# One-core attention and MLP kernel: the first head pair loaded by tokens, own buffers for q and k, a new order

## The chip, the cores and the metric

The kernel runs on one core of a Trainium2 chip. The metric is the device time of one execution in microseconds (us), taken on the chip; three executions give a median, 614.7 us before the change.

The engines are called by their profile names: PE multiplies matrices, PEld loads PE's stationary operand, DVE, ACT and POOL work element by element, and SP issues nearly all transfers (DMAs). PE writes to PSUM, a small memory of eight banks, from which only ACT and DVE copy.

## The reference

Causal attention over 4 batches x 12 heads x 448 tokens x 64, then a two-layer MLP on the 1792 tokens:

```
scores = q @ k.T / 8, masked above the diagonal
attn   = exp(scores - rowmax) / (rowsum + 1e-9)
x      = (attn @ v), heads side by side            # 1792 x 768, f32
h      = x @ w_in                                  # 768 x 2048
g      = where(h >= 1, h, where(h <= -1, 0, (h + 1)**2 / 4))
out    = g @ w_out                                 # 2048 x 768
```

q, k and v arrive as f32, w_in and w_out as 64-bit floats. The kernel narrows each weight from its two 32-bit words, splits it into a high and a low part and multiplies in three passes. Likewise it splits x and g.

## The kernel before

**Work.** Heads are taken in pairs, 24 of them (4 batches x 6), numbered 0 to 23. For a pair, *prep_pair* loads q and k and turns them so that the 64 head dimensions lie on partitions; *pair* makes the scores on PE (line L820, "S", 28 records of the profile), masks them and takes the row minimum on DVE (L839), takes exp on ACT (L843), scales by the reciprocal sum on POOL, ACT or DVE (L752, L754, L755), transposes the result on PE (L768, "T", 16 records) into a PSUM tile *t*, copies that to *pt* on ACT or DVE (L791, L796), and multiplies by v (L868, "V", 16 records). The result is split into x on ACT and DVE (L471, L480). The seven row tiles of a pair are called e6 (the widest) to e0.

The first MLP layer (*mlp1*, L617) needs the six x tiles of a batch. It runs in triples (the three passes for one block f of 128 columns and one x tile), 96 per batch and 384 in all, between the attention steps of the following batch. Its results pass through ACT (L627), DVE (L630) and either DVE (L636) or POOL (L633, L634) into *r* and are stored to DRAM. Only two *h* banks hold them. The second layer (L984) comes last, 1176 matmuls.

**Weights.** Each block of w_in comes in two transfers of 384 KB, 32 in all, into four raw buffers that are reused. ACT (L500) and DVE (L503, L505) decode, and a split on ACT, DVE or POOL follows. w_out is decoded during the attention, stored to DRAM and read back.

**The first pair.** PE starts with 18 fill matmuls on zeros (L894) and runs 7 more after the first scores. q and k of a pair are each loaded by four DMAs: 32 partitions, 3456 contiguous bytes each, where two bands of 32 dimensions are read by two overlapping loads, so each byte comes twice. A 32x32 transpose on DVE (L718) then makes the 64-row layout. The buffers for these loads are two *st* tiles, shared with the last w_in blocks. Pair 1 uses two early tiles of its own.

**What sets the order.** Nothing is ordered by hand. A planner (*Plan*) holds a list of tasks with costs, dependences and buffers. It simulates the engines with its own cost figures (*mm*, *act*, *dve*, *dma*), and after a first ranking it replays a list of seeds (STEPS), each of which shakes the priorities, the PE order or the engine chosen for some tasks. What comes out is the fixed order of every engine and of SP's queue. Each engine takes its instructions strictly in that order, so one that waits holds up all behind it. SP's transfers too are issued in order: one that waits for a buffer holds back the later ones.

Of the kernel before, what the change touches and what calls it, by code (L numbers as in the profile page):

```python
# [49 lines left out]
class Plan:  # L50
# [99 lines left out]
    def solve(self):  # L150
# [4 lines left out]
        for ahead in (14.0,):  # L155
            for pen in (0.1,):
# [204 lines left out]
def kernel(  # L361
# [9 lines left out]
    nc = tc.nc  # L371
# [23 lines left out]
    EVEN = 5  # L395
    NSTG = 2
# [8 lines left out]
        "w": 2 * KF, "st": 2, "sr": 2, "wn": 4, "x": 9, "r": 3, "vv": 1, "h": 2,  # L405
        "qs": 4, "vr": 2, "pt": 2,
        **{f"p{i}": 1 for i in range(NI)}, 
        "mn": 4, "su": 4, "s": 4, "t": 2,
        "w2": 8, "z": 2, "hl": 3, "w3": 10, "ot": 2,
# [12 lines left out]
    open_pools(base, "w st sr wn")  # L422
# [4 lines left out]
    open_pools(attn, "qs vr pt mn su")  # L427
# [28 lines left out]
    plan = Plan(slots, {"st", "t"})  # L456
# [52 lines left out]
    def parts(u):  # L509

        if isinstance(u, list):
            return [(x, 0, lambda x=x: x.tile) for x in u]
        if u.tag == "st":
            return [(u, z, lambda z=z: u[:, z * W2:(z + 1) * W2]) for z in range(2)]
        return [(u, z, lambda z=z: u[:, z]) for z in range(2)]
# [20 lines left out]
    def load_w_in(f, behind):  # L536
        w = wi[f] = [buf("w", [P, 2, W2], F32R) for _ in range(2)]
        for c, u in enumerate(w):
            src = w_in[c * K2 * P:(c + 1) * K2 * P, f * 2 * P:(f + 1) * 2 * P]
            if f < KF - NSTG:  # L540
                raw, claim = raw_in(stages[(2 * f + c) % len(stages)]), []
            else:
                raw, claim = raw_in(buf("st", [P, ROW])), [(u, "to")]
# [38 lines left out]
    HOMES = ["w2"] * 8 + ["wn", "wn", "st", "st", "sr", "sr"] + ["w"] * 32 + ["w3"] * 10  # L582

    def unit():
# [3 lines left out]
        if tag == "st":  # L588
            return buf("st", [P, ROW], F32R)
# [20 lines left out]
    def mlp1(b, f, nom):  # L610
        h = buf("s" if b == B - 1 and f >= OPEN else "h", [P, 512])
        for kk in range(KD):
# [9 lines left out]
            task([("PE", mm(S, times=3), go)], 0.0,  # L622
# [76 lines left out]

    def prep_pair(b, p, prio):  # L700
# [3 lines left out]
        for g in range(2):  # L704
            t = head[g] if no == 1 else buf("st", [P, ROW])
            first = None
            for i in range(2):
                row = (q, k)[g][b, 2 * p + i]
                for z in range(2):
# [3 lines left out]
                             dma(32 * 2 * S * 4, 230.0 if no else 185.0), 0.465, lat=1.25 if no else 1.0, early=no == 0, writes=[(t, 2 * i + z)], behind=loads[-1:] if first is None else ())  # L713
# [3 lines left out]
        for g, t in enumerate(nat):  # L717
            task([("DVE", 0.81, lambda g=g, t=t: nc.vector.transpose(  # L718
# [344 lines left out]
```

## Time and profile before

| | us |
|---|---|
| median of 3 runs (lowest, highest) | 614.7 (613.19, 617.15) |
| the profiled execution's own time | 615.45 |
| its span, first to last instruction | 613.6 |
| PE busy | 590.1 |
| DVE busy | 459.7 |
| ACT busy | 311.6 |
| POOL busy | 186.6 |

The span is what the trace covers. The execution's own time is 1.85 us longer, and it lies 0.75 us above the median. A row of a timeline gives start, length, engine, line and operation of a merged group, and in brackets the idle time of the engine before it with what ended it. Matmuls overlap in their pipeline, so the time that PE loses is read from its idle brackets and from the starts of successive groups, and the busy share says little.

### The profile page before, as it was taken

Reading aid. Unit: us, or ns where it says so; the run is one execution under the profiler, and the core shown is the slowest. Engines: PE = TensorE matmul, PEld = TensorE weight load, DVE = VectorE, ACT = ScalarE, POOL = GpSimd, SP = SyncE. Lnnn points to the kernel's source line nnn. Section 1 sums busy time; section 2 is a strip of 40 time slices with the busy share of each in tenths; the row PEclk is TensorE's granted clock in tenths of the full one; section 3 lists DMA queues with packets and bytes.
Section 4 is the critical chain, followed back from the end, with each engine's and each line's share of the span. In section 5 each row is a group of like instructions: output and inputs, shape, how many; then the busy total and the mean of one; then the engine's idle time right before and its main releaser. Section 6 shows DMA issues by size and latency. Waiting matters only on the chain.

```text
span 613.6 us, 11591 instructions
## 1 busy us (share of the span) xinstructions
PE 590.1 (96%) x3793; PEld 512.5 (84%) x3793; DVE 459.7 (75%) x1211; ACT 311.6 (51%) x784; POOL 186.6 (30%) x249
## 2 busy tenths in 40 slices
PE   8887999998999999999999999999999999999997
PEld 5555788776787787687787789999999999999997
DVE  5997999979847876968466779979766676655664
ACT  4997876848525655946356648444212222312221
POOL 2334563464433234120636323451021000032200
PEclk9999999999999999999999999999999999999999
DMA  8767898665887877767776369746323232423331
GB/s 206 220 191 201 249 261 258 179 177 164 209 287 217 277 228 218 193 217 220 206 237 187 99 201 348 241 138 207 107 76 122 75 120 73 135 76 114 91 100 67
DMA packets 96588, 110.33 MB, mean 180 GB/s; under 512 B 33552, under 2 KB 86288, under 8 KB 96528
## 3 DMA queue, kind: packets, MB, share of 16 engines
q1 hardware_dynamic: 96336, 109.15, 59.7%
q8 instruction: 30, 0.49, 0.3%
q10 hardware_dynamic: 192, 0.44, 0.2%
q14 instruction: 30, 0.25, 0.1%
HBM read 78.36 MB, written 31.20 MB: 179 GB/s over the span
## 4 chain that ended last, share of the span: by engine, by line
PE 47%; POOL 2%; DVE 1%; ACT 0%; issue 0%; POOLq 0%; ACTq 0%; DVEq 0%
PE s L984 17%; PE s L617 8%; PE h L984 8%; PE t L984 8%; PE h L617 3%; PE t L768 1%; PE t L868 1%; POOL r L633 1%; POOL r L634 1%; ACT e L843 0%; DVE vv L630 0%; DVE x L480 0%; DVE s L839 0%; PE s L820 0%; POOL su L849 0%
## 5 line engine op out<-in xcount | busy, mean ns | idle before, releaser
L617 PE MATMUL h<-x,w 128*128 128x448 f32 x900 | 204.4, 373 | 3.1 <-DVE vv L630 2.9
L617 PEld LDWEIGHTS h<-x,w 128*128 128x128 f32 x900 | 161.4, 188 | 18.3 <-DVE vv L630 6.1
L471 ACT ACTIVATE hl<-z 128x896 fp32r<-128x896 f32 x49 | 46.7, 952 | 120.7 <-DVE z L480 96.5
L984 PE MATMUL s<-w,hl 128*128 128x384 f32 x534 | 101.3, 335 | 0.0
L984 PEld LDWEIGHTS s<-w,hl 128*128 128x128 f32 x534 | 93.5, 188 | 0.1
L843 ACT ACTIVATE e<-s,mn 128x320 f32<-128x320 f32 (+6 forms) x168 | 78.4, 475 | 29.0 <-DVE mn L839 27.6
L480 DVE TENSOR_TENSOR hl<-z,hl 128x896 fp32r<-128x896 f32 x53 | 58.2, 1099 | 45.3 <-ACT hl L471 40.7
L839 DVE CUSTOM_DVE_ANT_0 s<-s,mask 128x320 f32<-128x320 f32 (+6 forms) x168 | 67.9, 445 | 6.7 <-PE s L820 3.2
L768 PE MATMUL t<-ident,e 128*128 128x128 f32 (+1 forms) x384 | 58.8, 278 | 11.7 <-ACT pt L791 4.7
L768 PEld LDWEIGHTS t<-ident,e 128*128 128x128 f32 (+1 forms) x384 | 43.0, 139 | 26.3 <-POOL e L752 6.3
L480 DVE TENSOR_TENSOR z<-z 128x128 f32<-128x128 f32 x199 | 56.5, 318 | 9.5 <-DMA z<-g_scratch 5.5
L630 DVE TENSOR_TENSOR vv<-h,r 128x448 f32<-128x448 f32 x50 | 31.0, 619 | 40.3 <-ACT r L627 25.2
L627 ACT ACTIVATE r<-h,half 128x448 f32<-128x448 f32 x50 | 31.5, 634 | 51.8 <-PE h L617 45.4
L481 POOL TENSOR_TENSOR z<-z 128x128 f32<-128x128 f32 x25 | 13.1, 524 | 137.2 <-DVE z L480 62.4
L868 PE MATMUL t<-pt,vr 128*64 128x448 f32 (+3 forms) x384 | 50.1, 391 | 3.7 <-ACT e L843 2.1
L984 PE MATMUL h<-w,hl 128*128 128x384 f32 x258 | 52.8, 335 | 0.0
L984 PE MATMUL t<-w,hl 128*128 128x384 f32 x258 | 52.6, 335 | 0.0
L633 POOL TENSOR_SCALAR r<-r 128x448 f32<-128x448 f32 x20 | 36.2, 1808 | 52.7 <-DVE vv L630 51.9
L617 PE MATMUL s<-x,w 128*128 128x448 f32 x252 | 51.8, 363 | 0.0
L868 PEld LDWEIGHTS t<-pt,vr 128*64 128x64 f32 (+1 forms) x384 | 23.9, 135 | 32.8 <-issue 19.9
L617 PEld LDWEIGHTS s<-x,w 128*128 128x128 f32 x252 | 47.0, 188 | 3.0
L984 PEld LDWEIGHTS h<-w,hl 128*128 128x128 f32 x258 | 45.5, 188 | 0.0
(93 smaller groups left out, 840.8 us busy)
## 6 DMA issues: line engine op xcount, KB each, us to landing
g_scratch<-r SPq DMA_DIRECT2D x64, 224.0 KB, 2.9
z<-g_scratch SPq DMA_DIRECT2D x56, 256.0 KB, 2.8
sr<-in_moe_w_out_dram SPq DMA_DIRECT2D x32, 384.0 KB, 4.2
w<-in_moe_w_in_dram SPq DMA_DIRECT2D x28, 384.0 KB, 5.0
w_scratch<-wn SPq DMA_DIRECT2D x56, 192.0 KB, 3.5
st<-in_q_dram SPq DMA_DIRECT2D x90, 108.0 KB, 2.7
st<-in_k_dram SPq DMA_DIRECT2D x90, 108.0 KB, 2.9
w<-w_scratch SPq DMA_DIRECT2D x50, 192.0 KB, 4.1
```

The source lines that it names most:

```text
L471: "ACT": ("ACT", act(n, 0.04), lambda: nc.scalar.activation(out=dst(), in_=src(), func=ACTF.Copy)),
L480: "DVE": ("DVE", dve(n), lambda: nc.vector.tensor_tensor(out=dst(), in0=x(), in1=y(), op=op), port),
L481: "POOL": ("POOL", pool_tt(n), lambda: nc.gpsimd.tensor_tensor(out=dst(), in0=x(), in1=y(), op=op), True),
L617: nc.tensor.matmul(out=h[:, :S], lhsT=wi[f][kk // K2][:, a, kk % K2 * P:(kk % K2 + 1) * P], rhs=x[:, c], start=(kk == 0 and n == 0), stop= ...
L627: task([("ACT", act(S, 0.1), lambda: nc.scalar.activation(out=r.tile, in_=h[:, :S], func=ACTF.Relu, scale=0.5, bias=half[:, 0:1]))], g0, r ...
L630: task([("DVE", dve(S), lambda: nc.vector.tensor_tensor(out=y.tile, in0=h[:, :S], in1=r.tile, op=ALU.max))], g0, reads=[(h, 0), (r, 0)], w ...
L633: nc.gpsimd.tensor_scalar(out=r.tile, in0=r.tile, scalar1=1.0, scalar2=1.0, op0=ALU.min, op1=ALU.mult)
L768: nc.tensor.transpose(t[:k, c:c + P], es[i][:, j * P:j * P + k], turners[i in SWAPPED])
L839: task([("DVE", dve(n) + (0.05 if n < 384 else 0.02), lambda s=s, off=off, n=n, i=i: nc.vector.tensor_tensor_reduce(out=s[:, off:off + n], ...
L843: task([("ACT", act(n, 0.19), lambda s=s, off=off, n=n, i=i: nc.scalar.activation(out=es[i][:, :n], in_=s[:, off:off + n], func=ACTF.Exp, ...
L868: nc.tensor.matmul(out=o[64 * g:64 * g + 64, j * P:S], lhsT=vr[:k, j, g, :], rhs=pt[:k, 7 * j:5 * j + NI, g, :] if j < NJ - 1 else pt[:k, ...
L984: nc.tensor.matmul(out=acc[x][:, :NO], lhsT=hl[:, a, i * P:(i + 1) * P], rhs=(hi, lo)[c](), start=(f == 0 and n == 0), stop=(f == KF - 2 a ...
```

## The change

Pair 0 (LIGHT = 1) now loads q and k by tokens: two DMAs each of 128 partitions x 4 x 64 elements, each run 256 bytes. Four transposes on PE for q and four for k (L729 of the changed kernel) put the layout into PSUM, and a copy on ACT or DVE (L732, L733) brings it to SBUF. q and k have four buffers of their own (*sq*), *vr* has three instead of two, *st* is gone; the last w_in blocks use *sr*, and two more w_out units lie in the pool *w2*. Some PE cost figures of the planner and its two search settings differ, and the list of seeds is another one, so the order of every engine is new.

```diff
-        for ahead in (14.0,):
-            for pen in (0.1,):
+        for ahead in (22.0,):
+            for pen in (0.4,):
...
     STEPS = (
-        5000004, 5000005, 5000008, 5000014, 5000017, 5000026, 5000027, 5000036, 5000038, 5000043, 5000066,
...
+        5000008, 5000011, 5000014, 5000017, 5000022, 5000033, 5000036, 5000051, 5000059, 5000060, 5000097,
...
+    LIGHT = 1
+    LEAD = 2.0
...
-        "w": 2 * KF, "st": 2, "sr": 2, "wn": 4, "x": 9, "r": 3, "vv": 1, "h": 2,
-        "qs": 4, "vr": 2, "pt": 2,
+        "w": 2 * KF, "sr": 2, "wn": 4, "x": 9, "r": 3, "vv": 1, "h": 2,
+        "sq": 4, "qs": 4, "vr": 3, "pt": 2,
...
-        "w2": 8, "z": 2, "hl": 3, "w3": 10, "ot": 2,
+        "w2": 10, "z": 2, "hl": 3, "w3": 10, "ot": 2,
...
-    plan = Plan(slots, {"st", "t"})
+    plan = Plan(slots, {"sq", "t"})
...
-                raw, claim = raw_in(buf("st", [P, ROW])), [(u, "to")]
+                raw, claim = raw_in(buf("sr", [P, DM])), [(u, "to")]
...
-    HOMES = ["w2"] * 8 + ["wn", "wn", "st", "st", "sr", "sr"] + ["w"] * 32 + ["w3"] * 10
+    HOMES = ["w2"] * 10 + ["wn", "wn", "sr", "sr"] + ["w"] * 32 + ["w3"] * 10
...
-            task([("PE", mm(S, times=3), go)], 0.0,
+            task([("PE", mm(S - 6, times=3), go)], 0.0,
...
+    def tokens(t):
+        return t[:, :NJ * 2 * D].rearrange("p (j g d) -> p j g d", g=2, d=D)
+
     def prep_pair(b, p, prio):
...
-            t = head[g] if no == 1 else buf("st", [P, ROW])
+            t = head[g] if no == 1 else buf("sq", [P, ROW])
...
+                if no < LIGHT:
+                    one = dma_task(lambda i=i, t=t: tokens(t)[:, :, i],
+                                   lambda row=row: bass.AP(row.tensor, row.offset, [[D, P], [P * D, NJ], [1, D]]),
+                                   dma(NJ * P * D * 4, 228.0), 0.5, lat=1.45, early=no == 0, writes=[(t, i)],
+                                   behind=loads[-1:] if first is None else ())
+                    first = first or one
+                    continue
...
         for g, t in enumerate(nat):
+            if no < LIGHT:
+                tb = buf("h" if no in (1, 2) or (no, g) == (0, 0) else "t", [P, 512])
+
+                def tr(t=t, tb=tb):
+                    for j in range(NJ):
+                        n = min(P, S - j * P)
+                        nc.tensor.transpose(tb[:, j * P:j * P + n], tokens(t)[:n, j].rearrange("p g d -> p (g d)"), ident[:n, :n])
+
+                task([("PE", mm(215, 110, P, NJ), tr)], prio, reads=[(t, 0), (t, 1)], writes=[(tb, 0)]).nom = at(no, "S", 6) - LEAD + 0.1 * g
+                task([("ACT", act(S, 0.04), lambda g=g, tb=tb: nc.scalar.activation(out=x[g].tile, in_=tb[:, :S], func=ACTF.Copy)),
+                      ("DVE", dve(S), lambda g=g, tb=tb: nc.vector.tensor_copy(out=x[g].tile, in_=tb[:, :S]))],
+                     prio, reads=[(tb, 0)], writes=[(x[g], 0)])
+                continue
...
-            task([("PE", mm(2 * P, P, P, nt * nb), tr)], prio, reads=[(eb[i], 0) for i in ii],
+            task([("PE", mm(215, 110, P, nt * nb), tr)], prio, reads=[(eb[i], 0) for i in ii],
...
-            t = task([("PE", mm(4 * S, T, P, pair=True), qk)], prio, reads=[(x[0], 0), (x[1], 0)], writes=keys)
+            t = task([("PE", mm(4 * S - 24, T, P, pair=True), qk)], prio, reads=[(x[0], 0), (x[1], 0)], writes=keys)
...
-        t_pv = task([("PE", [x for j in range(NJ) for x in mm(4 * (S - j * P), D, min(P, S - j * P), pair=True)], pv)], prio,
+        t_pv = task([("PE", [x for j in range(NJ) for x in mm(4 * (S - j * P) + 80, D, min(P, S - j * P), pair=True)], pv)], prio,
```

**Place 1: PE at the program's head**, before. h, t and s are PSUM banks, x holds the first pairs' q and k, qs those of later ones.

```order
L894 MATMUL h<-x 128x512 x18
L820 MATMUL s<-x 64x448 x2
L820 MATMUL s<-x 64x384 x2
...
L820 MATMUL s<-x 64x128 x2
L894 MATMUL h<-x 128x512 x7
L768 MATMUL t<-ident,e_133 128x128 x3
```

The same place in the changed kernel:

```order
L912 MATMUL h<-x 128x512 x18
L729 MATMUL h<-ident,sq 128x128 x3
L729 MATMUL h<-ident,sq 128x64
L729 MATMUL t<-ident,sq 128x128 x3
L729 MATMUL t<-ident,sq 128x64
L838 MATMUL s<-x 64x448 x2
...
L912 MATMUL h<-x 128x512 x7
L838 MATMUL s<-qs 64x448 x2
```

Eight transposes now stand between the 18 fills and the first scores, and pair 1's first scores come before pair 0's first transposes of e.

**Place 2: ACT around the first refill of a raw weight buffer**, before; wn is a decoded weight, w_274 a raw buffer, x_847 the x tile of pair 4, pt_804 belongs to pair 5.

```order
L791 ACTIVATE pt_804<-t_803 128x3x128
L793 ACTIVATE pt_804<-t_803 64x128
L500 ACTIVATE wn_834<-w_274 128x384
L754 ACTIVATE e2_127<-e2_127,su_747 128x192
L471 ACTIVATE x_847<-t_813 128x448
L791 ACTIVATE pt_804<-t_843 128x3x128
L500 ACTIVATE wn_857<-w_279 128x384
```

The same place in the changed kernel (pt_857 belongs to pair 5, x_862 to pair 4):

```order
L861 ACTIVATE e2_127,su_788<-s_773,mn_785 128x192
L499 ACTIVATE wn_852<-w_232 128x384
L470 ACTIVATE x_862<-t_835 128x448
L809 ACTIVATE pt_857<-t_856 128x3x128
L811 ACTIVATE pt_857<-t_856 64x128
L499 ACTIVATE wn_879<-w_402 128x384
```

SP's queue ahead of that decode, in the changed kernel (sq_439 and sq_478 are pair 5's, sq_644 and sq_679 pair 7's):

```order
L462 DMA sq_439<-in_q_dram 32x864 x4
L462 DMA sq_478<-in_k_dram 32x864 x4
L462 DMA vr_543<-in_v_dram 128x4x64 x2
L462 DMA sq_561<-in_q_dram 32x864 x4
L462 DMA sq_593<-in_k_dram 32x864 x4
L462 DMA vr_621<-in_v_dram 128x4x64 x2
L462 DMA sq_644<-in_q_dram 32x864 x4
L462 DMA sq_679<-in_k_dram 32x864 x4
L462 DMA w_232<-in_moe_w_in_dram 128x3x256
L462 DMA w_402<-in_moe_w_in_dram 128x3x256
```

The decode ahead of pair 4's x copy was of the seventh w_in load, and is now of the fifth; q and k up to pair 7 stand ahead of that load.

**Place 3: PE where pair 14's scores stand**, before, the last two rows of S and the V of pair 13:

```order
L820 MATMUL s_2688<-qs_2292,qs_2275 64x128 x2
L868 MATMUL t_2705<-pt_2536,vr_2230 64x448 x2
L868 MATMUL t_2705<-pt_2536,vr_2230 64x320 x2
L868 MATMUL t_2705<-pt_2536,vr_2230 64x192 x2
L868 MATMUL t_2705<-pt_2536,vr_2230 64x64 x2
L617 MATMUL h_2646<-x_2191,w_1484 128x448 x3
```

In the changed kernel the V of pairs 12 and 13 stand together, and S of pair 14 behind them:

```order
L886 MATMUL t_2614<-pt_2294,vr_2002 64x448 x2
L886 MATMUL t_2614<-pt_2294,vr_2002 64x320 x2
L886 MATMUL t_2614<-pt_2294,vr_2002 64x192 x2
L886 MATMUL t_2614<-pt_2294,vr_2002 64x64 x2
L886 MATMUL t_2631<-pt_2393,vr_2211 64x448 x2
...
L886 MATMUL t_2631<-pt_2393,vr_2211 64x64 x2
L838 MATMUL s_2652<-qs_2217,qs_2199 64x448 x2
```

Over the whole program V and S stand more often side by side, and two pairs are under way at once.

## Rows read from the trace of the kernel before

**Rows 1.** Busy time by stretch; columns: stretch, length, PE, PEld, DVE, ACT, POOL, PEclk, DMA.

```profile
8.30:64.00 55.70, 46.39 (x430) 30.77 (x429) 48.84 (x174) 47.62 (x159) 21.88 (x45) 1.00 0.76 204
64.00:110.00 46.00, 45.45 (x281) 37.70 (x284) 43.99 (x101) 33.32 (x82) 22.59 (x25) 1.00 0.90 260
110.00:355.80 245.80, 237.14 (x1649) 188.17 (x1640) 184.78 (x555) 145.97 (x420) 92.30 (x115) 1.00 0.69 204
404.20:613.60 209.40, 205.86 (x1185) 205.42 (x1183) 135.83 (x299) 53.63 (x68) 30.23 (x37) 1.00 0.35 107
```

**Rows 2.** Timeline of PE, 0 to 27 us.

```profile
8.29 1.75 PE L820 MATMUL s<-x 64*64 64x448 f32 x28
...
13.34 0.98 PE L768 MATMUL t<-ident,e 128*128 128x128 f32 x7 [1.48 <-POOL e L752]
...
20.50 0.63 PE L768 MATMUL t<-ident,e 128*128 128x128 f32 x4 [0.16 <-PE t L868]
21.06 1.75 PE L820 MATMUL s<-qs 64*64 64x448 f32 x28
```

**Rows 3.** Fill matmuls in 3 to 5 us, then in 7 to 8.6 us: ns min/median/max.

```profile
L894 PE MATMUL h<-x x6: 628/628/628, 2.5 to 4.6; 128*128 128x512 f32 x6
...
L894 PE MATMUL h<-x x6: 388/389/507, 6.7 to 8.0; 128*128 128x512 f32 x6
```

**Rows 4.** Timeline of DVE and ACT, 0 to 16 us.

```profile
6.80 0.97 DVE L718 STREAM_TRANSPOSE x<-st 128x448 f32<-128x448 f32 x1 [1.15 <-DMA st<-in_k_dram]
...
10.14 0.64 ACT L843 ACTIVATE e<-s,mn 128x448 f32<-128x448 f32 x1 [6.27 <-DVE mn L839]
```

**Rows 5.** Two copies of ACT by shape, whole span: busy us, mean ns, idle before.

```profile
L791 ACT ACTIVATE pt<-t 128x384 f32<-128x384 f32 x50 | 24.0, 489 | 3.7 <-PE t L768 3.6
...
L471 ACT ACTIVATE x<-t 128x448 fp32r<-128x448 f32 x15 | 8.1, 541 | 4.1 <-PE t L868 4.1
```

**Rows 6.** Waits of ACT from 10 to 61 us: total, times, longest.

```profile
ACT e L843 <- DVE mn L839: 8.4, 5, 6.3
ACT wn L500 <- DMA w<-in_moe_w_in_dram: 3.3, 1, 3.3
```

**Rows 7.** Timelines of SP, ACT and PE around that wait.

```profile
48.95 0.98 SPq L463 DMA_DIRECT2D w<-in_moe_w_in_dram  x2
...
55.05 0.55 ACT L500 ACTIVATE wn<-w 128x384 f32<-128x384 f32 x1 [3.29 <-DMA w<-in_moe_w_in_dram]
...
61.06 1.24 PE L868 MATMUL t<-pt,vr 128*64 128x448 f32 x6 [0.18 <-ACT e L843]
```

**Rows 8.** Waits of PE from 64 to 356 us: total, times, longest.

```profile
PE h L617 <- DVE vv L630: 2.9, 5, 1.1
PE t L768 <- DVE e L755: 2.4, 5, 0.6
PE t L768 <- POOL e L752: 2.3, 2, 1.7
```

**Rows 9.** The chain of waits, 303 to 309 us: start, us.

```profile
303.65 1.89 POOL r L633
...
307.46 0.55 POOL e L752
```

**Rows 10.** Timeline of PE, 266 to 290 us.

```profile
268.44 0.60 PE L768 MATMUL t<-ident,e 128*128 128x128 f32 x4
268.79 2.67 PE L617 MATMUL h<-x,w 128*128 128x448 f32 x12
```

**Rows 11.** Weight loads issued from 60 to 110 us: KB each, median us to landing.

```profile
w<-in_moe_w_in_dram SPq DMA_DIRECT2D x19, 384.0 KB, 5.1
```

**Rows 12.** Timelines of SP and PE around the 24th weight load.

```profile
99.93 0.92 SPq L463 DMA_DIRECT2D w<-in_moe_w_in_dram  x2
...
111.28 3.08 PE L617 MATMUL h<-x,w 128*128 128x448 f32 x14
```

**Rows 13.** The chain of waits, the end of attention: start, us.

```profile
351.74 4.12 PE t L868 x32
```

More of the change, by code (lines that the diff above doesn't have):

```diff
@@ L421 @@
     const = base.enter_context(tc.tile_pool(name="const", bufs=1))
-    open_pools(base, "w st sr wn")
+    open_pools(base, "w sr wn")
     open_pools(base, "h s t", PSUM)
@@ L426 @@
     early = attn.enter_context(tc.tile_pool(name="early", bufs=1))
-    open_pools(attn, "qs vr pt mn su")
+    open_pools(attn, "sq qs vr pt mn su")
     g_dram = tc.dram_tile([KF, P, NT], F32, name="g_scratch")
@@ L512, in parts @@
             return [(x, 0, lambda x=x: x.tile) for x in u]
-        if u.tag == "st":
-            return [(u, z, lambda z=z: u[:, z * W2:(z + 1) * W2]) for z in range(2)]
         return [(u, z, lambda z=z: u[:, z]) for z in range(2)]
@@ L587, in unit @@
             return [buf(tag, [P, W2], F32R) for _ in range(2)]
-        if tag == "st":
-            return buf("st", [P, ROW], F32R)
         return (buf if tag in ("w", "sr") else bbuf if tag == "w2" else lbuf)(tag, [P, 2, W2], F32R)
@@ L712, in prep_pair @@
                              lambda row=row, z=z: bass.AP(row.tensor, row.offset + 32 * z, [[C * D, 32], [1, ROW]]),
-                             dma(32 * 2 * S * 4, 230.0 if no else 185.0), 0.465, lat=1.25 if no else 1.0, early=no == 0, writes=[(t, 2 * i + z)], behind=loads[-1:] if first is None else ())
+                             dma(32 * 2 * S * 4, 230.0), 0.465, lat=1.25, writes=[(t, 2 * i + z)], behind=loads[-1:] if first is None else ())
                     first = first or one
```

19 rows, old and new, of the table STEPS are left out of this document.

## Prediction

> **What bounds the kernel.** I read the busy time by stretch first. From 404.2 us to the end PE is busy 205.86 of 209.40 us, the rest being the last sums and stores: the second layer runs without a gap. From 110 to 355.8 us PE idles 8.7 us, from 64 to 110 us 0.6, but from 8.3 to 64 us 9.3 [rows 1]. So the kernel is bound by PE, whose work the change hardly touches, and what an order can win is some 18 us of idle time in two unlike parts. In the first, attention runs alone for six pairs, because the first layer needs all six x tiles of a batch; there DVE is busy 48.84 and ACT 47.62 of 55.70 us [rows 1], and PE waits for them. In the second, PE has the first layer to fill in, and its waits are single events of 0.3 to 1.7 us [rows 8]. I go through both and then look for what the new order puts at risk. S(n), T(n), V(n) are the scores, the transposes and the product by v of pair n.
>
> **The first scores.** What the reader should see at the head is that the transfers do not set S(0). The second 32x32 transpose ends at 6.80 + 0.97 = 7.77, but the 18 fills issue until about 8.2, the last starting at 8.0, and S(0) follows at 8.29 [rows 2 to 4]. Loading fewer bytes therefore gains nothing here, since the fills cover any landing before 8.2. The eight new transposes stand behind the fills. Seven e transposes took 0.98, so eight take about 1.1: 8.29 to 9.4, q's four done near 8.95. ACT makes both copies by the order, at 0.54 each [rows 5]: with handovers of about 0.18 (as before V at 61.06 [rows 7]) 9.1 to 10.2, and S(0) starts near 10.35. That is **+2.1 us**, between +1.5 (the copies hidden but for one) and +2.6. DVE loses two transposes of 0.97, and pair 1's two now run before S(0) instead of between pair 0's masks.
>
> **The first six pairs.** ACT starts its first exp at 10.14 [rows 4] and then hardly rests. From 10 to 61 us it waits 3.3 us once for a weight transfer, and for DVE 8.4 us, of which 6.3 lie before that first exp [rows 6]. ACT is the chain, and its first exp moves with S(0). By the order ACT issues 109 instructions up to its last pt copy for pair 5, before 101. Two are the new first copies, counted already; the other six are mostly pt copies taken over from DVE, 0.49 each [rows 5], +2.9 at most, and 0 at least, since the scalings kept on ACT are smaller ones. I take **+1.5**. Against that stands the wait of 3.29 us at 55.05: the weights were issued at 48.95, behind pair 6's k and a v load, and the decode stood in ACT's order ahead of pair 4's x copy, so x, then DVE, then T and V(5) at 61.06 came late [rows 7]. In the new queue this load stands behind pair 7's k, which waits only for pair 5's q and k to be turned; with four buffers pair 5's turning follows the masks of pair 3, one pair earlier than before, about 36 us by my count of DVE's work in the new order. The load should issue near 40 and land near 45 (5.1 to landing [rows 11]), while ACT reaches the decode past 52. So **-3.3**, bounded by 0, if the decode waits all the same. The other cheap edits (three v buffers, two units moved to another pool) act only through this queue. The start comes to +2.1 + 1.5 - 3.3 = +0.3: V(5) at about 61.4.
>
> **From there to the second layer.** In both orders 10 triples of the first layer precede S(7), so the rest can be compared piece by piece. (a) Entries to and exits from S and V, counted behind S(7): 53 before, 45 now. Four transposes before an S take 20.50 to 21.06 = 0.56, before a product of the first layer 268.44 to 268.79 = 0.35 [rows 2, 10]; a switch costs up to 0.21, eight 1.7. But T and the first layer alternate eight times more often, which I bound by 0 and 0.1 each. **-1.0**, between -1.7 and 0. (b) The h banks. PE waited 2.9 us for DVE's vv [rows 8], which frees a bank. I counted the PE work between a bank's last product and its reuse, at 0.2 us a matmul: under 2 us at 18 of 48 places before, at 11 of 49 now, and POOL's slow form of the last step (20 before) is taken only 8 times. **-1.5**, between -2.5 and +1.5. (c) T waits 2.3 us for POOL's e and 2.4 for DVE's [rows 8]. The longest, 1.7, is a chain in which e6 stood behind r on POOL [rows 9]; fewer r help, but e6 goes to POOL 18 times instead of 8, and T of e5 now follows T of e6 at once. **-1.0**, between -2 and +2. The PE work from S to the first T stays 4.8 us or more.
>
> **The second layer** I cost at nothing. Its cover is the stretch from V(23), 351.74, to the first product near 404.2 [rows 1, 13], when the weights are read back. Behind V(23) now stand 74 triples instead of 83, at 0.61 each 5.5 us less of 52. If that were too short, the first products would wait a few us.
>
> **Sum.** +0.3 - 1.0 - 1.5 - 1.0 = -3.2 us on the span of 613.6, so 610.4. The profiled execution took 615.45, 1.85 more than its span and 0.75 above the median of 614.7; the change would take it to 612.25 and the median to **611.5 us**.
>
> [...]
>
> **Rivals.**
> 1. *The start gains more* (0.17). DVE has less to do up to pair 5, so ACT's other waits for it, 8.4 - 6.3 = 2.1 us, go too, and T's waits fall by half rather than a fifth (another -1.4, 4.7 in all): 611.5 - 3.5 = 608. For: ACT's work is the same kind in both. Against: the new ACT list is longer.
> 2. *The weights come late* (0.20), the case on the other side. By the order the 24th w_in load stands behind 24.4 MB of transfers in SP's queue, before behind 23.1 (each row's shape x 4 bytes). At 260 GB/s and DMA 0.90 busy [rows 1] 1.3 MB are 5 us. Its first product is now the triple just before S(8), near 64.3 + 46 = 110; before it was the fifth behind 111.28, at 113.7, against a landing at about 100.4 + 5.1 = 105.5 [rows 11, 12]. Without a lead it would land at 110.5, need some 3.5 us of decode and split, and PE would stand some 4 us; the waiting decode also blocks ACT in order, as at 55.05, 1 to 2 more. 611.5 + 5.2 = **616.7**. It decides if SP's queue at 64 us is less than about 4 us ahead of before. For: DMA is the fullest there. Against: the deeper q and k buffers let SP run ahead while DMA was only 0.76 busy [rows 1].
> 3. *The first pair loses* (0.10). The late S(0) and the longer ACT list stay, but the 3.3 us stall merely gives place to another: 614.8.
> 4. *The clock falls at the head* (0.03). [...] Against: it kept its level over the idle 1.48 us before 13.34.
>
> **Numbers.** The forecast has 0.50, with its terms' bounds 607.5 to 615.5. Eight in ten lie from **606.5 to 617.5**: below it only both gains of rival 1 with the best bounds, above it rival 2 twice over, or a late second layer. A median of this kernel tells from no change about 1%, 6.1 us. Faster by more, under 608.6: most of rival 1 and the forecast's lower edge, 0.21. Slower by more, over 620.8: rival 2 together with rival 3, 0.09. Within: 0.70.
>
> **What would show it.** S(0) at 10.3 and first exp near 12.2: the first term. No wait of ACT for w_in above 1 us before V(5), and V(5) at 60 to 62.5: the second. PE's wait for vv under 1.5 us and its idle time from S(7) to 356 near 6 us: (b) and (c). A PE wait behind a weight split between 85 and 115 us would mean rival 2, and a fill over 500 ns behind S(0) rival 4. A gap in the products after the first of L984's kind would break the cover I gave the second layer.

## The result and the profile after

| | before | after |
|---|---|---|
| median (lowest, highest) of four runs each, us | 614.85 (613.19, 617.15) | 607.72 (606.13, 609.14) |
| profiled execution: time, span | 615.45, 613.6 | 608.45, 606.7 |
| first exp on ACT | 10.14 | 11.70 |
| V(5) | 61.06 | 57.09 |
| S(7) | 64.00 | 59.83 |
| start of the last matmul | 609.72 | 602.90 |

The ratio is 0.9889, 95% interval 0.9854 to 0.9924: 7.1 us, just over 1%. The forecast was 611.5, in a range that holds 607.7; the time is that of rival 1 (608).

Busy time by stretch, to be laid beside [rows 1]: up to S(7), to 110, to the end of attention, and the second layer.

```profile
9.84:59.83 49.99, 46.91 (x429) 30.53 (x430) 44.23 (x158) 47.00 (x163) 20.75 (x46) 1.00 0.88 230
59.83:110.00 50.17, 46.69 (x266) 40.10 (x265) 42.88 (x97) 32.98 (x80) 21.59 (x24) 0.97 0.84 253
110.00:353.50 243.50, 237.79 (x1685) 193.35 (x1683) 186.25 (x539) 151.25 (x443) 71.08 (x113) 1.00 0.68 204
397.40:606.60 209.20, 205.08 (x1180) 204.38 (x1179) 140.56 (x310) 54.70 (x68) 21.58 (x35) 1.00 0.34 105
```

PE idled 9.3 us up to S(7) before and idles 3.1 now. From there to 110 us it was nearly always busy (0.6 idle), and now idles 3.5; the granted clock, 0.97, tells of a fall. Of the 6.8 us by which the last matmul starts earlier, 4.2 are there at S(7). S(7) before, then V(5) and S(7) after (V(5) before stands in [rows 7]):

```profile
64.00 0.99 PE L820 MATMUL s<-qs 64*64 64x448 f32 x12
```

```profile
57.09 2.10 PE L886 MATMUL t<-pt,vr 128*64 128x448 f32 x16 [0.16 <-ACT pt L809]
59.83 1.75 PE L838 MATMUL s<-qs 64*64 64x448 f32 x28
```

Two rows tell how: busy time from the first exp to V(5), first before, then after (columns as in [rows 1]).

```profile
10.14:61.06 50.92, 41.87 (x381) 28.02 (x382) 45.27 (x162) 44.72 (x147) 19.29 (x40) 1.00 0.76 205
```

```profile
11.70:57.09 45.39, 42.37 (x382) 27.87 (x382) 41.90 (x152) 44.26 (x152) 19.65 (x43) 1.00 0.88 229
```

ACT, the fourth figure, works as long as before (44.26 and 44.72 us), but in 45.39 us instead of 50.92: its idle time falls from 6.20 to 1.13. DVE has 3.4 us less to do, and DMA is busier, 0.88 for 0.76. ACT's waits from 10 to 61 us, to be laid beside [rows 6]:

```profile
ACT e L861 <- DVE mn L857: 2.3, 3, 1.9
```

Of these 2.3 us, 1.9 lie before the first exp. The row for w_in is gone: no decode waits for its weights in this stretch. SP issues three loads, the fifth to the seventh, in one group:

```profile
44.61 1.45 SPq L462 DMA_DIRECT2D w<-in_moe_w_in_dram  x3
```

The fifth lands at 49.48 and ACT decodes it at 51.49. The seventh is issued at 45.62 and lands at 52.37 (before: issued at 48.95 [rows 7], landed at 54.97). The head, PE and then ACT:

```profile
1.44 6.56 PE L912 MATMUL h<-x 128*128 128x512 f32 x18 [1.44 <-DVE x L905]
7.83 0.70 PE L729 MATMUL h<-ident,sq 128*128 128x128 f32 x4
8.46 0.75 PE L729 MATMUL t<-ident,sq 128*128 128x128 f32 x4
9.84 1.75 PE L838 MATMUL s<-x 64*64 64x448 f32 x28 [0.63 <-ACT x L732]
```

```profile
8.57 0.54 ACT L732 ACTIVATE x<-h 128x448 f32<-128x448 f32 x1 [5.44 <-PE h L729]
9.25 0.54 ACT L732 ACTIVATE x<-t 128x448 f32<-128x448 f32 x1
11.70 0.64 ACT L861 ACTIVATE e<-s,mn 128x448 f32<-128x448 f32 x1 [1.91 <-DVE mn L857]
```

S(0) takes 1.75 us as in [rows 2], so the clock held (PEclk 1.00 up to S(7)). Behind S(7) the waits of PE from 64 to 356 us, beside [rows 8]:

```profile
PE h L612 <- DVE vv L625: 4.3, 2, 3.0
PE t L786 <- ACT e L772: 2.6, 2, 1.7
PE t L786 <- DVE pt L814: 0.7, 1, 0.7
PE t L786 <- POOL e L770: 0.5, 1, 0.5
```

The longest wait of the kernel is new. ACT, then PE, then the busy time by stretch around it:

```profile
65.21 0.55 ACT L499 ACTIVATE wn<-w 128x384 f32<-128x384 f32 x1 [2.00 <-DMA w<-in_moe_w_in_dram]
65.66 0.51 ACT L470 ACTIVATE w<-wn 128x384 fp32r<-128x384 f32 x1
66.07 1.14 ACT L622 ACTIVATE r<-h,half 128x448 f32<-128x448 f32 x2
```

```profile
67.40 4.86 PE L612 MATMUL h<-x,w 128*128 128x448 f32 x15 [3.03 <-DVE vv L625]
```

```profile
66.00:68.00 2.00, 0.60 (x2) 0.56 (x3) 1.28 (x4) 2.00 (x6) 0.99 (x1) 0.89 0.87 225
68.00:70.00 2.00, 2.00 (x7) 1.80 (x6) 2.00 (x7) 2.00 (x7) 0.23 (x1) 0.50 1.08 367
70.00:72.00 2.00, 2.00 (x9) 1.82 (x9) 1.67 (x9) 1.47 (x4) 1.93 (x3) 0.76 1.00 257
```

It is the stall of before in another place. The ninth w_in load, issued at 59.94, lands at 65.18; ACT's decode waits for it in its order, the two r stand behind the decode, vv behind r, and PE needs the bank that vv frees. After 3.03 us of idle time PEclk falls to 0.50, and the first ten products take 3.69 us (67.40 to 71.09) where ten at the full clock take 2.0 (elsewhere in after twelve took 2.66 at 176.11 and eighteen 3.86 at 171.11, so 0.2 each): another 1.7 us.

### The profile page after: what moved, and what is told of

Read it like the earlier page. It is cut to its first block, busy times and chain, and to the rows that moved or that the text cites. A ratio compares the mean times of both kernels' runs of the same rounds, so it can differ in the third digit from the quotient of the medians.

```text
span 606.7 us, 11566 instructions
## 1 busy us (share of the span) xinstructions
PE 588.1 (97%) x3801; PEld 515.4 (85%) x3801; DVE 454.0 (75%) x1183; ACT 318.0 (52%) x811; POOL 147.5 (24%) x238
## 4 chain that ended last, share of the span: by engine, by line
PE 77%; DVE 11%; ACT 5%; DMA 2%; issue 2%; POOL 1%; SPq 0%; DVEq 0%; ACTq 0%
PE h L612 24%; PE s L1002 17%; PE h L1002 8%; PE s L612 8%; PE t L1002 8%; DVE s L857 4%; PE t L786 4%; PE t L886 4%; ACT e L861 3%; PE s L838 2%; DVE qs L736 2%; DMA vr<-in_v_dram 1%; PE h L912 1%; DVE wn L504 1%; DVE mn L857 1%
## 5 line engine op out<-in xcount | busy, mean ns | idle before, releaser
L612 PEld LDWEIGHTS h<-x,w 128*128 128x128 f32 x900 | 163.6, 190 | 18.8 <-DVE vv L625 5.5
L1002 PE MATMUL s<-w,hl 128*128 128x384 f32 x552 | 104.7, 335 | 0.8 <-DVE vv L625 0.8
L1002 PEld LDWEIGHTS s<-w,hl 128*128 128x128 f32 x552 | 96.6, 188 | 1.1 <-DVE vv L625 1.1
L479 DVE TENSOR_TENSOR hl<-z,hl 128x896 fp32r<-128x896 f32 x54 | 60.4, 1119 | 49.2 <-ACT hl L470 43.8
L479 DVE TENSOR_TENSOR z<-z 128x128 f32<-128x128 f32 x198 | 51.7, 292 | 5.7 <-DMA z<-g_scratch 2.4
L1002 PE MATMUL h<-w,hl 128*128 128x384 f32 x270 | 55.4, 335 | 0.0
L1002 PE MATMUL t<-w,hl 128*128 128x384 f32 x270 | 55.2, 335 | 0.0
L770 POOL TENSOR_SCALAR e<-e,su 128x448 f32<-128x448 f32 (+6 forms) x74 | 42.9, 584 | 44.1 <-DVE su L872 36.7
L809 ACT ACTIVATE pt<-t 128x384 f32<-128x384 f32 (+2 forms) x94 | 44.3, 492 | 9.6 <-PE t L786 9.5
L1002 PEld LDWEIGHTS t<-w,hl 128*128 128x128 f32 x270 | 47.6, 188 | 0.0
```

The lines of the kernel that those rows point to most:

```text
L479: "DVE": ("DVE", dve(n), lambda: nc.vector.tensor_tensor(out=dst(), in0=x(), in1=y(), op=op), port),
L612: nc.tensor.matmul(out=h[:, :S], lhsT=wi[f][kk // K2][:, a, kk % K2 * P:(kk % K2 + 1) * P], rhs=x[:, c], start=(kk == 0 and n == 0), stop= ...
L770: ("POOL", pool_ts(n, 0.09), lambda: nc.gpsimd.tensor_scalar(out=ev(), in0=ev(), scalar1=sc(), scalar2=1.0, op0=ALU.mult, op1=ALU.mult), T ...
L809: nc.scalar.activation(out=dst(), in_=src(), func=ACTF.Copy)
L1002: nc.tensor.matmul(out=acc[x][:, :NO], lhsT=hl[:, a, i * P:(i + 1) * P], rhs=(hi, lo)[c](), start=(f == 0 and n == 0), stop=(f == KF - 2 a ...
```

## The experiments

The theory after the comparison: what carries the change is that ACT, in its fixed order, no longer waits for weights and for DVE in the first six pairs, and this reaches the end one to one (A). Its rivals: the tokens carry it (B), the shorter steps behind S(7) carry it, and what is won at the start is lost again behind it (C).

In all runs the order of every engine was held fixed as recorded from one of the two kernels, and only the named places changed (line numbers as before or after). E1, e2, e4 and e5 ran together, so did e6 to e9, and e10 to e12, and e13 alone; each session has its own runs of before, with medians of 613.5 to 614.4.

| run | median us | ratio to before | 95% interval |
|---|---|---|---|
| e1_decode_later | 615.77 | 1.0032 | 1.0013 to 1.0052 |
| e5_own_buffers_only | 618.08 | 1.0071 | 1.0051 to 1.0092 |
| e6_own_qk_buffers | 612.70 | 0.9968 | 0.9947 to 0.9989 |
| e12_tokens_on_before | 617.49 | 1.0060 | 1.0040 to 1.0081 |
| e8_after_again | 608.11 | 0.9908 | 0.9880 to 0.9936 |
| e2_first_pair_by_bands | 609.95 | 0.9934 | 0.9908 to 0.9960 |
| e11_bands_fills_between | 610.27 | 0.9928 | 0.9901 to 0.9955 |
| e13_bands_full_clock | 608.93 | 0.9912 | 0.9882 to 0.9942 |
| e7_thirteen_fills | 605.97 | 0.9879 | 0.9844 to 0.9914 |
| e4_r_before_decode | 605.72 | 0.9875 | 0.9854 to 0.9896 |
| e9_waits_filled | 604.60 | 0.9851 | 0.9824 to 0.9877 |
| e10_fills_between_t | 604.56 | 0.9859 | 0.9833 to 0.9885 |

**Is the stall at 55 us on the path?** E1 moves the decode in the order of before.

```diff
 ACT
-L500 ACTIVATE wn<-w 128x384
 L754 ACTIVATE e_127<-e_127,su 128x192
 L471 ACTIVATE x<-t 128x448
 ...
 L791 ACTIVATE pt<-t 128x2x2x128
+L500 ACTIVATE wn<-w 128x384 x2
 L843 ACTIVATE e_132,su<-s,mn 128x384
```

> The order of before, kept word for word but for one place: ACT's decodes of the 7th and 8th w_in load, and the three operations on DVE and POOL that follow the first of them, stand behind pair 5's pt copies instead of ahead of pair 4's x copy. Theory A (ACT's wait of 3.29 us for that load, in its order, was on the path to the end): the wait for w_in falls under 0.5 us, V(5) comes at about 57.8 instead of 61.06, S(7) at about 60.8 instead of 64.00, and the time is about 3.3 us under before, 611.5. Rival (the wait only covered others: DVE and T would be late anyway): V(5) stays at 60 or later and the time within 1 us of before, 614 to 615.

V(5) came at 57.14, but S(7) at 62.79 and the end 1.6 us late. Of the 3.9 us at V(5), 0.5 were there at S(0) already (7.76 instead of 8.29), since the first fill that took under 0.6 us started at 5.44 in this execution and at 6.72 in before. PE from 57 us:

```profile
57.14 2.10 PE L868 MATMUL t<-pt,vr 128*64 128x448 f32 x16
62.21 0.66 PE L768 MATMUL t<-ident,e 128*128 128x128 f32 x4 [2.96 <-POOL e L752]
```

My edit had left the rest of the weight's work on DVE and POOL ahead of pair 6's e6. DVE did its part from 58.67 to 60.02, and the reciprocal that e6 needs stood behind it, at 59.93. POOL waited for DVE until 60.10 and made the weight's low part before e6. Behind PE's wait of 2.96 us the six products from 63.71 took 2.51 us instead of e6's 1.48, and the mean granted clock of this execution was 0.996 (before: 1.000). So the run shows the first half of theory A (the wait off ACT, V(5) 3.4 earlier) and not the second: the wait went to the next engines that had the weight in their lists.

**The buffers alone.** E5 gives the order of before all new buffers; e6 gives it only q's and k's.

```diff
 e6
-        "qs": 4, "vr": 2, "pt": 2,
+        "sq": 4, "qs": 4, "vr": 2, "pt": 2,
-            t = head[g] if no == 1 else buf("st", [P, ROW])
+            t = head[g] if no == 1 else buf("sq", [P, ROW])
 e5: these, "vr": 3, "st" gone, its raw tiles in "sr", its two units in "w2"
```

> The order of before on every engine and queue, but with the buffers of the change: four of their own for q and k, three for v, the two units moved. Theory A1 (the buffers alone free SP's queue): q and k loads no longer wait for DVE's transposes of the pair before, the 7th w_in load is issued at 45 or earlier instead of 48.95, ACT's wait of 3.29 us falls under 1 us, V(5) near 58, time about 611.5. Rival A2 (the order decides: in this queue the load stands behind the same q, k and v loads, and the transfers are no faster): load issued at 47 or later, wait over 2 us, time 613.5 to 615.

> The order of before on every engine and queue, with four buffers of their own for q and k and nothing else: the raw w_in and w_out tiles and the two weight units keep the buffers of before (in the run with all new buffers V(5) came at 57.40 and S(7) at 60.34, 3.7 us early, but a wait of ACT for a raw w_out tile near 141 us gave back 6.3). Theory A1 (own buffers for q and k alone take away the wait for the 7th w_in load, and what is won there reaches the end when no other load is late): V(5) near 57.4, S(7) near 60.3, no wait of PE over 2 us behind them, time 3.7 us under before, near 610.5. Rival A2 (what is won up to S(7) is lost behind it whatever the buffers, since the first layer's weights come when DMA brings them): V(9) within 1 us of 155.9, time 613.5 to 615.

In both the stall went, with the order unchanged: V(5) at 57.40 and 57.89, S(7) at 60.34 and 60.84 (0.5 us of e5's lead were there at S(0), as in e1); in e6 the load was issued at 45.05 instead of 48.95. PE of e6:

```profile
57.89 2.10 PE L868 MATMUL t<-pt,vr 128*64 128x448 f32 x16
60.84 0.99 PE L820 MATMUL s<-qs 64*64 64x448 f32 x12
```

A1 holds up to there. In e5 the lead was lost at 145 us, in the same manner: the raw tiles of the last w_in and of w_out now shared two buffers, and ACT waited in its order for one of them. E6, which leaves these tiles as they were, has no such wait. ACT and PE of e5:

```profile
145.49 0.54 ACT L500 ACTIVATE wn<-sr 128x384 f32<-128x384 f32 x1 [6.12 <-DMA sr<-in_moe_w_out_dram]
```

```profile
147.17 1.51 PE L768 MATMUL t<-ident,e 128*128 128x128 f32 x6 [6.29 <-ACT pt L791]
```

In e6 3.16 us at S(7) became 2.6 at the V that stood at 155.9 before, 3.5 at the one at 337.2, 2.3 at the next, and 2.0 at the last matmul: 1.7 in the median, half of A1's figure. The largest loss, 1.2 us, has a place. Two of DVE's decode operations, POOL beside them, and then PE, in e6:

```profile
335.28 1.15 DVE L503 TENSOR_SCALAR wn<-wn 128x384 uint32<-128x384 uint32 x1
336.46 1.24 DVE L505 SCALAR_TENSOR_TENSOR wn<-sr,wn 128x384 uint32<-128x384 uint32 x1
```

```profile
335.06 2.23 POOL L481 TENSOR_TENSOR wn<-wn 128x384 f32<-128x384 f32 x2 [1.02 <-DMA w_scratch<-wn]
```

```profile
342.02 0.92 PE L768 MATMUL t<-ident,e 128*128 128x128 f32 x6 [1.24 <-DVE e L755]
```

The same two took 0.35 and 0.56 us before, where POOL's operation came behind them, and T waited 0.31. In these two traces such operations took at most 0.57 us where POOL did not work beside them for most of their time, and up to 1.41 where it did. This is read from the traces; no run moves POOL's operation alone.

**The first pair by tokens alone.** E12 puts it into the order and buffers of before (the diff of *prep_pair* with LIGHT = 1, pair 1's DVE transposes ahead of pair 0's masks).

> The order and the buffers of before; only the first pair's q and k come by tokens and are turned on PE, with ACT's two copies, and pair 1's two DVE transposes stand ahead of pair 0's masks, as in the change. Theory H (the tokens by themselves only put the start later): S(0) at 9.8 instead of 8.29, first exp at 11.7, V(5) 1 to 1.5 later than 61.06, time 615.5 to 616.5. Theory L (four loads and 0.36 MB fewer at the head of the queue bring every later load forward by about 1 us, the 7th w_in load too, and DVE has two transposes fewer): V(5) at 60.5 or earlier, time 613 to 614.

S(0) came at 10.08, V(0) to V(4) were 1.7 to 1.8 late. The stall shrank to 1.5 us, mostly because ACT came to it 1.8 later; the seventh load was issued later too (50.73) and landed 0.45 earlier (54.52). So V(5) stood at 60.69 and S(7) at 63.57. But V(23) was 2.0 late and the time 3.1 over before. The first four w_in loads were issued 0.5 earlier, the fifth to the seventh 1.7 to 2.1 later, so theory L fails on the loads and on the time. Theory H fails at V(5), and the time is 1 us beyond its range: alone, this part loses.

**The first pair by bands in the new order.** E2, e11 and e13 take the tokens out of after and differ only in their fills.

```diff
-    LIGHT = 1
+    LIGHT = 0
 e2: 7 fills behind S(0); e11: 3 there, 1 + 1 + 2 + 2 between T of pair 0 and ahead of V(0)
 e13: 8 there, 2 + 2 + 2
```

> The order of after, but the first pair's q and k come by bands and are transposed on DVE, as before; the eight PE transposes and ACT's two copies are gone, pair 1's k is transposed behind pair 0's masks. Theory A (the first pair by tokens only costs 1.5 us of start, the gain comes from later): S(0) at 8.3 instead of 9.84, first exp at 10.1 instead of 11.70, V(5) near 55.6 instead of 57.09, time about 1.5 us under after, 606.2. Theory B (the tokens carry the gain, since they take two transposes of 0.97 us from DVE, which is nearly full up to pair 5): V(5) at 57.5 to 59, time 608 to 610.

> The order of after with the first pair by bands, as in the run before, where the granted clock fell to 0.50 at 20 to 22 us and V(5) came 2.0 late; now with the same six fills between pair 0's transposes and ahead of V(0). Theory K (1.6 of those 2.0 us were the clock, the first pair by tokens itself is worth 0.4 at most): granted clock 1.00 from 16 to 24 us, V(5) near 57.5, time within 1 us of after. Theory B (the tokens carry it, by DVE's two transposes and four loads fewer on SP ahead of all others): V(5) at 58.5 or later even at the full clock, time 1.5 to 3 over after.

> The order of after with the first pair by bands, a third time: eight fills behind S(0), and two each ahead of three of pair 0's transposes and of V(0), so that PE is not left to transposes and waiting (with seven fills behind S(0) the granted clock was 0.50 at 20 to 22 us, with three there and six later it was 0.50 at 14 to 16 us). Theory K (the clock was what the bands lost; the first pair by tokens itself is worth little): granted clock 1.00 from 10 to 24 us, V(0) at 19.4 to 19.9 taking 2.1, V(5) at 57.0 to 57.5, time within 1 us of after, 607 to 608.5. Theory B (the tokens carry something themselves, by DVE's two transposes and the loads that come 0.8 us earlier): V(5) at 58 or later at the full clock, time 609 or more.

S(0) came at 7.65 to 8.12, first exp near 9.9, and yet V(5) at 59.09, 58.13 and 57.80 against 57.09 with tokens. In e2 PE ran V(0) at the lower clock (PEclk 0.50 from 20 to 22 us):

```profile
19.91 3.73 PE L886 MATMUL t<-pt,vr 128*64 128x448 f32 x16 [0.50 <-ACT pt L809]
```

It takes 2.10 at the full clock (at 19.39 in after), so 1.6 of e2's 2.0 us were the clock. E11 lost it earlier, at 14 to 16 us (PEclk 0.50). E13 kept 1.00 from 8 to 66 us and was still 0.7 late at V(5): from the first exp to there DVE waited 2.1 us for loads of q and k, 0.2 in after. V(5) and the time lie between the figures of theories K and B, so neither is shown; the time is that of after. In this order, then, the tokens cost 1.8 us at the first exp (11.70 against 9.90) and give back 2.5 by V(5), and a difference of 0.7 is too small for the medians.

**An earlier start.** E7 and e10.

```diff
-    WARM = 18
+    WARM = 13
 e10: also e9's order, and 3 fills behind S(0), 1 + 1 + 2 + 2 between T of pair 0 and ahead of V(0)
```

> The order of after with 13 fills ahead of the first transposes instead of 18. They end near 6.7 instead of 7.83, the last k load of pair 0 lands at 5.96, so S(0) comes near 8.75 instead of 9.84 and the first exp near 10.6. Theory L (behind S(0) the loads of pairs 1 to 3, issued one behind the other on SP, pace the first pairs): S(1) gains 0.5 at most, V(1) within 0.3 of 26.55, time within 0.7 us of after. Rival A (ACT's chain of exps starts earlier and stays ahead): V(5) 1.0 earlier, near 56.0, time 1 us under after. If the clock has not risen when the fills end, S(0) takes 1.75 us or more and nothing is won.

> The order with the waits filled, 13 fills ahead of the first transposes instead of 18, and of the seven fills behind S(0) four stand between pair 0's transposes and ahead of V(0), two of them doubled (1 + 1 + 2 + 2). With 13 fills alone S(1) came 1.75 us early, but the granted clock of 20 to 22 us was 0.50 and V(0) took 3.73 us instead of 2.10, so that S(2) came 0.9 late. Theory K (only that fall of the clock, behind a stretch in which PE did little but transposes and wait, ate the earlier start): granted clock 1.00 from 16 to 24 us, V(0) takes 2.1, S(2) at about 21.3, V(5) near 56.4, time 0.7 under the kernel with the waits filled, near 603.9. Rival D (DVE and ACT are full there and hold S(2) at 22 anyway): S(2) at 21.9 or later, V(5) at 57, time 604.5 or more.

S(0) came at 8.20 in e7, so the fills do set it. Then neither theory held: PE of e7 and one row of its busy time.

```profile
16.08 1.12 PE L786 MATMUL t<-ident,e 128*128 128x128 f32 x7 [0.39 <-issue]
17.81 0.41 PE L786 MATMUL t<-ident,e 128*128 128x128 f32 x2 [0.61 <-DVE pt L814]
18.72 3.73 PE L886 MATMUL t<-pt,vr 128*64 128x448 f32 x16 [0.51 <-ACT pt L809]
22.97 1.75 PE L838 MATMUL s<-qs 64*64 64x448 f32 x28
```

```profile
20.00:22.00 2.00, 2.00 (x10) 0.71 (x6) 1.57 (x5) 1.42 (x6) 1.62 (x4) 0.50 1.01 237
```

From 16.08 PE does transposes and waits, then V(0) runs at a PEclk of 0.50 and takes 3.73 us, and S(2) stands 0.96 later than in after. It was a near thing: after has almost the same stretch, without the wait of 0.39, and kept 1.00:

```profile
18.49 0.41 PE L786 MATMUL t<-ident,e 128*128 128x128 f32 x2 [0.62 <-DVE pt L814]
19.39 2.10 PE L886 MATMUL t<-pt,vr 128*64 128x448 f32 x16 [0.50 <-ACT pt L809]
```

Whether the transposes or the idle time between them took e7's clock down is not shown, since no run here parts the two. In e10, with fills in that stretch (PEclk 1.00 from 14 to 72 us):

```profile
18.68 2.10 PE L886 MATMUL t<-pt,vr 128*64 128x448 f32 x16
...
21.40 1.75 PE L838 MATMUL s<-qs 64*64 64x448 f32 x28
```

Theory K holds for the clock and S(2), but V(5) at 56.87 gained only 0.4 on e9's 57.24, and the time is e9's, as rival D has it. The first exp came 0.9 earlier (10.73), and ACT's listed waits for DVE and loads between it and V(5) grew from 0.9 to 1.4 us. E7's own median is not separate from that of e8; its six runs lie between 603.2 and 610.0.

**The new stall at 65 us.** E4 changes the order of after.

```diff
 ACT
+L622 ACTIVATE r<-h,half 128x448 x2
 L499 ACTIVATE wn<-w 128x384
 L470 ACTIVATE w<-wn 128x384
-L622 ACTIVATE r<-h,half 128x448 x2
 DVE
+L625 TENSOR_TENSOR vv<-h,r 128x448
 L857 ISA s,mn<-s,mask 128x448
 ...
 L857 ISA s,mn<-s,mask 128x384
-L625 TENSOR_TENSOR vv<-h,r 128x448
```

> The order of after, but for one place: ACT makes r of the two full h banks ahead of the decode of the 9th w_in load and the split copy, not behind them, and DVE makes the first vv ahead of two masks of pair 7. Theory A (an ACT that waits in its order for a weight load costs PE here as it did at 55 us in before, and the lower clock behind the wait costs again): PE's wait of 3.03 us for vv at 67.40 falls under 1 us, the granted clock of 66 to 70 stays at 1.00 instead of 0.69, and the time falls by 2 (wait) to 4 us (wait and clock), to 603.7 to 605.7. Rival (ACT is the chain here too, and the two r only put pair 7's masks and exps later): PE waits as long for e or pt of pairs 6 and 7, and the time stays at 607 to 608.

> The order of after, unchanged, on the same chip as the other three, to compare with. Every theory expects a ratio to before of 0.989 within 0.003, near 607.5 us.

PE and busy time of e4:

```profile
64.63 2.08 PE L612 MATMUL h<-x,w 128*128 128x448 f32 x9 [0.51 <-DVE vv L625]
67.56 1.45 PE L612 MATMUL h<-x,w 128*128 128x448 f32 x6 [0.86 <-ACT pt L809]
```

```profile
68.00:70.00 2.00, 2.00 (x14) 1.79 (x13) 1.97 (x12) 1.36 (x3) 1.60 (x2) 1.00 1.12 326
```

The wait of 3.03 became 0.51 and 0.86, the clock stayed at 1.00, and S(7) to the last matmul took 540.15 us instead of 543.07 (before: 545.72). The intervals of e4 and e8 overlap a little, because the stall is not the same in every execution: in e8, the unchanged program, it was 2.3 us and the clock held (PEclk 1.00 from 60 to 76 us), and that stretch took 541.27. PE of e8:

```profile
65.88 3.31 PE L612 MATMUL h<-x,w 128*128 128x448 f32 x15 [2.32 <-DVE vv L625]
```

So theory A is shown in the traces, at 1.1 to 2.9 us, and not in the medians.

**All waits behind S(7).** E9 is e4 with six more places changed; one of them:

```diff
 PE, pair 22
 L612 MATMUL h<-x,w 128x448 x15
+L612 MATMUL h<-x,w 128x448 x9
 L786 MATMUL t<-ident,e_133 128x128 x3
 L786 MATMUL t<-ident,e_133 64x128
-L612 MATMUL h<-x,w 128x448 x3
 ...
```

> The order with r ahead of the decode at 65 us, and six more places changed: ahead of four waits of T (0.63 at 142, 0.89 at 200, 0.78 at 214, 1.71 at 328 us) stand one, one, one and three triples of the first layer that stood behind them; and at two places DVE makes vv ahead of masks and a transpose, where PE waited 0.86 at 67.6 and 1.26 at 161.7 for the bank. Theory P (from S(7) to the second layer PE is the bound, so each wait that is filled comes off the end): PE's waits from 64 to 356 us fall from 7.5 to about 2.5, time 4 to 5 us under the kernel with r ahead of the decode, 601 to 602. Rival C (T and with it ACT's and DVE's chain come later and the waits return at the next T or V): time 604.5 to 606.

PE of e9 from 321 us, then its longest waits from 64 to 356 us:

```profile
321.08 5.07 PE L612 MATMUL h<-x,w 128*128 128x448 f32 x24
326.07 0.99 PE L786 MATMUL t<-ident,e 128*128 128x128 f32 x7
```

```profile
PE t L786 <- ACT e L772: 1.4, 2, 1.1
PE h L612 <- DVE vv L625: 0.7, 2, 0.5
```

Idle time over 0.12 us behind S(7) fell from 9.4 (e8) to 3.6, and the last matmul came 3.6 earlier, at 597.44. The other 2.2 us of idle time came back in short delays between steps. Against e4, whose order it extends, idle time fell from 8.0 to 3.6 and S(7) to the last matmul from 540.15 to 537.58: some 60% of a filled wait comes off the end. That is theory P in part. The median lies 1.1 us under e4's, in rival C's range and with overlapping intervals, so what the six places add is not shown in the medians. At 604.6 against 608.1 for after and 614.4 for before in the same session, e9 beats both, and its interval lies under that of e8.

## Why the prediction was right, and where it was not

The range and the direction held. The size did not: -3.2 was forecast, -7.1 measured, and the likeliest case was no measurable change. Up to V(5) the forecast was 4.3 us too high, 2.0 of it in ACT's list, 1.8 in ACT's other waits and 0.5 in S(0). Behind S(7) it looks close, -3.5 against -2.65, but by luck: idle time rose by 0.8 where (b) and (c) had it fall by 2.5, and the steps lost 3.5 where (a) had 1.0. Rival 1's 608 is met in part by luck too, since only one of its halves came. By the prediction's own terms:

- **S(0), +2.1**: +1.55. From the first new transpose to S(0) it took 2.01 us, where I had 2.06: mechanism right. Pair 0's last k load landed at 5.96, ahead of the fills' end. The missing 0.5 is luck: the same 18 fills gave way at 7.83 instead of 8.29, since the first fill that took under 0.6 us started at 5.87 instead of 6.72.
- **ACT's list, +1.5: wrong.** From the first exp to V(5) ACT ran 152 instructions instead of 147, but was busy 44.26 us instead of 44.72: -0.5. Counting each up to the start of the next, pt copies came to +2.5, scalings to -1.8, decodes and splits to -0.7 and the same exps, closer together, to -0.8. I had counted the copies taken over from DVE and not what ACT gave up.
- **The stall, -3.3**: gone, as forecast, but with a margin of 2.0 us instead of 7: the load that the decode ahead of pair 4's x copy needs was issued at 44.61 and landed at 49.48, not near 40 and 45, and ACT decoded it at 51.49. E6 shows that q's and k's buffers alone do it.
- **ACT's other waits**: I let them stand, and this step failed. ACT's idle time behind the first exp fell by 5.07 us, 3.3 for the weights and 1.5 of the rest for DVE, whose work there fell by 3.4. This is rival 1's mechanism; its other half, T's waits falling by half, did not come (see (c)). Together the start came to 1.55 - 5.07 - 0.46 = -3.98 at V(5), where I had +0.3.
- **(a) switches, -1.0**: mis-sized. Adding up the time from each matmul's start to the next behind S(7), without idle time over 0.12 us, gives 536.7 before, 533.2 after (1.7 of it the lower clock at 67.4) and 531.9 in e8. Products of the first layer that delayed their successor beyond 0.25 us were 130, 108 (ten of them at the lower clock) and 98 in number. By kind of step, e8 against before: product to product -1.9, transpose to transpose -1.7, product to scores -1.5. I had counted entries to S and V only, and left out the many delays too short to be listed as waits.
- **(b) h banks, -1.5: wrong in sign**, 2.9 to 4.3. The count of places with little cover was right in kind (without the stall at 65 us one wait of 1.3 is left), but 3.0 us came from one decode that stood ahead of r on ACT (e4).
- **(c) T, -1.0**: right in size, by another way. T's waits fell from 5.6 to 4.2 with the small ones; those of [rows 8] for an e of POOL and of DVE became 0.5 and none, but ACT's e now takes 2.6.
- **PE's idle time from S(7) to 356** was 9.1, as before (9.0), not near 6.
- **Second layer at nothing**: one wait of 0.76 at 402.07, for vv and not for weights. (The row in [rows 13] holds two V; the last starts at 353.77, which shortens the cover by 2 us and changes nothing.)
- **Rival 2** named the right danger, a decode that waits for its load and blocks ACT; it came at the ninth load, at 65 us, not at the 24th. **Rival 4** did not come at S(0) (1.75 us, PEclk 1.00); in e7, e2 and e11 PEclk fell to 0.50 between 14 and 22 us, so the head was close to it.

What the change consists of does not add up from its parts: q's and k's buffers alone give -1.7, all the new buffers +4.0, the tokens alone +3.1, the new order and buffers without tokens -4.1 to -4.6 (e2, e11, e13), the whole -6.2 to -7.1. The rest comes with the order, which was searched with these parts in place; no run gives the new order the old buffers, so its share is a remainder and not a measurement. Theory A holds for the first six pairs, but not one to one: e6 kept 2.0 of 3.2 us, as rival C has it in part. Which moves of the order gave the shorter steps behind S(7) is not settled.

## What to carry to other kernels

On engines that work strictly in order, ask of every instruction that waits for a transfer what stands behind it, on its own engine and on the next ones that handle the same data: a late weight cost 3.3 us on ACT, 3.0 of PE's time behind DVE and POOL (e1), and another 6.3 through a shared buffer (e5). Compare an engine's busy time with the length of the stretch from its first to its last link before counting its instructions. An earlier start is worth only what the engines behind it can take, and it can turn into a loss if PE's clock falls behind it (in e7 1.6 us earlier at S(0), PEclk 0.50 under V(0), 0.8 later at V(5)).

## What the hardware showed that I had not expected

A wait of PE cost more than its length where the clock fell: 3.03 us of idle time cost 1.7 us more in after. But the length of the wait did not tell whether it fell. Before the same products PE waited 2.2 us in e7 and 2.8 in e11, and PEclk was 0.52 and 0.50 from 68 to 70 us; it waited 2.3 in e8, where PEclk stayed at 1.00, and 3.2 in e2, where the fifteen products took 3.28 us against 4.80 in e7:

```profile
66.58 4.80 PE L612 MATMUL h<-x,w 128*128 128x448 f32 x15 [2.21 <-DVE vv L625]
```

```profile
68.93 3.28 PE L612 MATMUL h<-x,w 128*128 128x448 f32 x15 [3.22 <-DVE vv L625]
```

The first row is e7's, the second e2's. After and e8 are one program, so two of its executions differ by that. The fills differ too: of the same 18 at the head the first that took under 0.6 us started at 6.72 us in before, 5.87 in e5 and 5.44 in e1, and S(0) at 8.29, 7.82 and 7.76. In before and after the fills go from 628 to 389 ns with PEclk at 1.00 throughout, so what quickens them is not shown. At the head, transposes with waits of 0.39, 0.61 and 0.51 us among them ended in the lower clock in e7 (PEclk 0.50 from 20 to 22 us), while e10, with six fills in that stretch, kept the full clock (1.00). I had taken the level, once reached, for safe.
